# GpSimd takes the smaller of two scores for even groups too, ScalarE writes the queries' high part, the per-pair work stands elsewhere

## Chip, core and metric

One core of a Trainium2 chip runs the whole program. The metric is the device time of one execution in microseconds (us); several executions were timed, and another one was profiled.

## What is computed

Three stages follow one another. The change lies in the first, attention in which each query keeps only its 32 largest scores:

```python
def _attn_ref(q, k, v):                      # q, k, v: (4, 8, 576, 64)
    scores = scale * np.matmul(q, k.transpose(0, 1, 3, 2))
    kth = np.partition(scores, -32, axis=-1)[..., -32:-32 + 1]
    scores = np.where(scores >= kth, scores, -1000000000.0)
    attn = np.exp(scores - np.max(scores, axis=-1, keepdims=True))
    attn = attn / (np.sum(attn, axis=-1, keepdims=True) + 1e-09)
    return np.matmul(attn, v)
```

Its output goes token by token to one of eight experts (`h = max(x @ w1[e], 0)`, `out = gate * (h @ w2[e])`), and then through one dense layer pair with a piecewise quadratic function in between. Those two stages are untouched.

## The kernel before

The 32 heads are taken in 16 pairs. A pair has nine score tiles ("units") of 128 queries by 576 keys, so there are 144 units, worked off in 72 groups g of two. Each pass of the loop over g (L503) writes out, engine by engine, one group's selection (`topk`, L238), the masks and the product with v of the groups before it, and the scores of group g + 4 (`AHEAD`). Every engine runs its own instructions in the order in which they were written; only data and buffers make it wait.

**The selection.** VectorE finds the 32 largest of 576 with an instruction that gives the eight largest of a row (MAX8) and one that strikes these out (MATCH_REPLACE8). To shorten the rows, a *fold* (`fold`, L209) first halves them: `big` is the larger of column i and column i + 288 (L215), `c` the larger of the two halves of `big` (L216), `lit2` the smaller of them (L217). One fold serves four units, that is two groups: it is made in each odd group g for the groups g + 1 and g + 2. The smaller values of the first halving, `lit`, have two makers. For even groups VectorE makes them with one minimum (`smaller`, L222). For odd groups GpSimd does, as the exact integer sum of both columns (L230) less the larger one (L235); this is `less`, and a dependency written by hand lets it start only behind VectorE's L222. The groups of `DIRECT` keep VectorE. Then come three pairs of MAX8, over `lit2` (L253), over `lit` (L255) and over `c` with the best eight of each appended (L257), in an odd group the fold, and three rounds of MATCH_REPLACE8 (L266, its MATCH_VALUE_LOAD ahead of it) and MAX8 (L269). GpSimd makes the exponent's bias `nm` from the first maximum (L258) and copies two small results, `edge` and `top` (L242), when it comes to the next group.

**The per-pair work.** Scores are made from split operands, so each pair needs k and q transposed (`turn`, ScalarE copies kT and qT from PSUM, L170), the rounded high parts kh (VectorE, `kparts`, L174) and qh (GpSimd, `qparts`, L182), and the rests kl and ql (GpSimd, `krest` L178, `qrest` L186). `prep` sets the groups: turns in g - 2, kh in g - 1, the rest in g, with g odd (L393): 3, 7, 13, 17, 21, 25, 31, 35, 39, 43, 49, 53, 57, 61; the work of pair 1 stands in group 0. TensorE multiplies with them from L197 to L199, and ScalarE evacuates a unit's scores with L207.

**The output of a pair** (`xout`, L338) is scaled by VectorE's L343 and L344 and a product on GpSimd, in the odd groups 7, 11, 17, 21, 25, 29, 35, 39, 43, 47, 53, 57 and 61 for the first 13 pairs. In groups 66 to 68 GpSimd scatters token rows to DRAM (five, five and three).

Of the kernel before, what the change touches and what calls it, by code (L numbers as in the profile page):

```python
# [11 lines left out]
AF = mybir.ActivationFunctionType  # L12
ALU = mybir.AluOpType
# [33 lines left out]
AHEAD = 4  # L47
LEAVE = 3
START = (0, 1, 1, 2, 2, 3)
DIRECT = (67, 71)  # L50
FIRST = (0, 4, 9, 13)
NT1 = FIRST[B - 1]
SEG = ((0, 512), (512, S))
# [12 lines left out]
class Kernel:  # L66
# [32 lines left out]
    def attention(self, moe):  # L99
        nc, tc = self.nc, self.tc  # L100
        with ExitStack() as ctx:
            P = self.P
# [11 lines left out]
            def nb(n):  # L114
                return n if P.deep else 1
# [21 lines left out]
            raw, kq, st, xr = {}, {}, {}, {}  # L137
# [5 lines left out]
            def load(j, other=nc.sync):  # L143
                for nm, src, queue in (("k", self.k, nc.sync), ("q", self.q, other)):
                    t = raw[nm, j] = P.kq.tile([128, 5, 2, D], F32, name="r" + nm, bufs=nb(2))
                    for i, hd in enumerate(heads(src, j)):
                        queue.dma_start(t[:, 0:4, i, :],
                                          hd[:, :, 0:512, :].rearrange("a b (p c) d -> p (a b c) d", c=4))
                        queue.dma_start(t[0:64, 4, i, :],
                                          hd[:, :, 512:S, :].rearrange("a b p d -> p (a b d)"))  # L150

            def load_v(j, t):
                for i, hd in enumerate(heads(self.v, j)):
                    nc.sync.dma_start(t[:, i, 0:4, 0:D],
                                      hd[:, :, 0:512, :].rearrange("a b (p c) d -> p (a b c) d", c=4))
                    nc.sync.dma_start(t[64:128, i, 4, 0:D],
                                      hd[:, :, 512:S, :].rearrange("a b p d -> p (a b d)"))

            def vtile(j):
                return P.V[j % len(P.V)]  # L160

            def turn(j, nm):
                r = raw.pop((nm, j))
                p = P.sp.tile([128, 1024], F32, name="sp")
                for c in range(5):
                    n = 128 if c < 4 else 64
                    nc.tensor.transpose(p[:, c * 128:c * 128 + n],
                                        r[:n, c].rearrange("p h d -> p (h d)"), self.ident[:n, :n])
                t = kq[nm, j] = P.kq.tile([128, S], F32, name=nm + "T", bufs=nb(2))
                nc.scalar.activation(t, p[:, :S], AF.Copy)  # L170

            def kparts(j):
                hi = kq["kh", j] = P.kq.tile([128, S], F32R, name="kh", bufs=nb(2))
                nc.vector.tensor_copy(hi, kq["k", j])  # L174

            def krest(j, eng=nc.gpsimd):
                lo = kq["kl", j] = P.kq.tile([128, S], F32R, name="kl", bufs=nb(2))
                eng.tensor_tensor(lo, kq["k", j], kq["kh", j].bitcast(F32), op=ALU.subtract)  # L178

            def qparts(j):  # L180
                t, (hi, lo) = kq["q", j], P.Q[j % len(P.Q)]
                nc.gpsimd.tensor_tensor(hi, t[:, 0:512], P.zero, op=ALU.add)  # L182

            def qrest(j, eng=nc.gpsimd):
                t, (hi, lo) = kq["q", j], P.Q[j % len(P.Q)]
# [23 lines left out]
            def fold(s):  # L209
                h, q = S // 2, S // 4  # L210
                n = s.shape[1]
                big = P.wk.tile([128, n, h], F32, name="big", bufs=1)
                c = P.wk.tile([128, n, q + 16], F32, name="c")
                lit2 = P.wk.tile([128, n, q], F32, name="lit2", bufs=1)
                nc.vector.tensor_tensor(big, s[:, :, 0:h], s[:, :, h:S], op=ALU.max)  # L215
                nc.vector.tensor_tensor(c[:, :, 0:q], big[:, :, 0:q], big[:, :, q:h], op=ALU.max)  # L216
                nc.vector.tensor_tensor(lit2, big[:, :, 0:q], big[:, :, q:h], op=ALU.min)  # L217
                return [[t[:, i:i + 2] for t in (c, lit2, big)] for i in range(0, n, 2)]

            def smaller(g):  # L220
                lits[g] = P.wk.tile([128, 2, S // 2], F32, name="lit")
                return nc.vector.tensor_tensor(lits[g], st[g][:, :, 0:S // 2], st[g][:, :, S // 2:S], op=ALU.min)  # L222

            folded, lits, moved = {}, {}, []

            def less(g, behind):

                i = st[g].bitcast(I32)
                t = P.wk.tile([128, 2, S // 2], I32, name="lit")
                d = nc.gpsimd.tensor_tensor(t, i[:, :, 0:S // 2], i[:, :, S // 2:S], op=ALU.add)  # L230

                tc.add_manual_dep(d.ins, behind.ins.name,
                                  mybir.DependencyInfo(mybir.DependencyClass.Sync, mybir.DependencyReason.DATA),
                                  reason="shared port")
                nc.gpsimd.tensor_tensor(t, t, folded[g][2].bitcast(I32), op=ALU.subtract)  # L235
                lits[g] = t.bitcast(F32)

            def topk(g):  # L238
                q = S // 4
                two = range(2)  # L240
                while moved:
                    nc.gpsimd.tensor_copy(*moved.pop(0))  # L242
                if g < 2:
                    folded[g], = fold(st[g])
                if g not in lits:
                    smaller(g)
                c, lit2, _ = folded.pop(g)
                lit = lits.pop(g)
                m8 = P.wk.tile([128, 2, TOPK // 8, 8], F32, name="m8", bufs=4)
                z = P.wk.tile([128, 2, q + 16], F32, name="z", bufs=1)  # L250
                nm = P.wk.tile([128, 2], F32, name="nm", bufs=4)
                for i in two:
                    nc.vector.max(c[:, i, q + 8:q + 16], lit2[:, i])  # L253
                for i in two:
                    nc.vector.max(c[:, i, q:q + 8], lit[:, i])  # L255
                for i in two:
                    nc.vector.max(m8[:, i, 0], c[:, i])  # L257
                nc.gpsimd.tensor_scalar(nm, m8[:, :, 0, 0], -0.125, None, op0=ALU.mult)  # L258
                if g % 2 and g + 1 < ng:
                    folded[g + 1], folded[g + 2] = fold(four[g // 2 + 1])  # L260
                    behind = smaller(g + 1)
                    if g + 2 not in DIRECT:
                        less(g + 2, behind)
                for r in range(TOPK // 8 - 1):
                    for i in two:
                        nc.vector.match_replace(out=z[:, i], in_to_replace=m8[:, i, r],  # L266
                                                in_values=c[:, i] if r == 0 else z[:, i], imm_value=LOWEST)
                    for i in two:
                        nc.vector.max(m8[:, i, r + 1], z[:, i])  # L269
                last = m8[:, :, TOPK // 8 - 1, 7:8]  # L270
                moved.append((edge[:, 2 * g:2 * g + 2], c[:, :, q + 7::8]))
                moved.append((top[:, 2 * g:2 * g + 2], last[:, :, 0]))
                return [(last[:, i], nm[:, i:i + 1]) for i in two]
# [88 lines left out]
            ng = nu // 2  # L362
            later = {}

            def at(g, f, *a):
                later.setdefault(max(g, 0), []).append((f, a))

            def odd(g):
                return g if g % 2 else g - 1

            def prep(j, g, *eng):

                at(g - 2, turn, j, "k")
                at(g - 2, turn, j, "q")
                at(g - 1, kparts, j)
                at(g, krest, j, *eng)
                at(g, qparts, j)
                at(g, qrest, j, *eng)

            load(0, nc.scalar)  # L380
# [9 lines left out]
            at(1, self.route_consts)  # L390
            at(5, self.route_consts2)
            for j in range(1, len(pairs)):
                g = odd(9 * j // 2 - AHEAD - 1)  # L393
                prep(j, g)
                if j + 1 < len(pairs):
                    at(g - 2, load, j + 1)
# [191 lines left out]
            def again(j):  # L588
                load(j)
                load_v(j, vtile(j))  # L590
                for nm in "kq":
                    turn(j, nm)
                kparts(j)
                krest(j)
                qparts(j)
                qrest(j)
                for u in range(9):
                    s = P.wk.tile([128, S], F32, name="s1", bufs=1)
                    sevac(s, qk(j, u))
                    t, nm = topk_plain(s)  # L600
                    work = [(j, u, ptevac(pt(ex(s, nm), wmask(s, t))))]
                    avevac(work, av(work))
                xout(j)
# [1136 lines left out]
```

## Time and profile before

| | |
|---|---|
| median of 3 timed runs | 1214.36 us (1214.07 to 1219.26) |
| profiled execution, its own time | 1211.65 us |
| its span, first to last instruction | 1210.0 us |
| mean granted TensorE clock | 0.962 of full speed |
| busy: TensorE, VectorE, ScalarE, GpSimd | 1119.0, 842.0, 693.8, 499.6 us |
| attention | up to some 515 us |

A row of the timeline gives the start, the duration and the instruction; in brackets stands how long its engine had been idle before it, and what ended that. "x2" merges two instructions of a kind. Consecutive instructions of VectorE overlap by some 0.08 us, so what one costs its queue is the step from its start to the next start. A duration also holds the time in which an instruction that had been issued was held up.

### The profile page before, as it was taken

Reading aid. Unit: us, or ns where it says so; the run is one execution under the profiler, and the core shown is the slowest. Engines: PE = TensorE matmul, PEld = TensorE weight load, DVE = VectorE, ACT = ScalarE, POOL = GpSimd, SP = SyncE. Lnnn points to the kernel's source line nnn. Section 1 sums busy time; section 2 is a strip of 40 time slices with the busy share of each in tenths; the row PEclk is TensorE's granted clock in tenths of the full one; section 3 lists DMA queues with packets and bytes.
Section 4 is the critical chain, followed back from the end, with each engine's and each line's share of the span. In section 5 each row is a group of like instructions: output and inputs, shape, how many; then the busy total and the mean of one; then the engine's idle time right before and its main releaser. Section 6 shows DMA issues by size and latency. Waiting matters only on the chain. (4 is left out here: it accounts for less than half of the span.)

```text
span 1210.0 us, 24589 instructions
## 1 busy us (share of the span) xinstructions
PE 1119.0 (92%) x8900; PEld 955.7 (79%) x8901; DVE 842.0 (70%) x2572; ACT 693.8 (57%) x1230; POOL 499.6 (41%) x621
## 2 busy tenths in 40 slices
PE   8987989899989898777999999889899999999997
PEld 5776878677878776666888787778799999999996
DVE  6999999999999999886757888477422232322222
ACT  4878888898889886733655544345333333333322
POOL 2555556555555555752224445132232322222221
PEclk7899999999999998997999999899899999999999
DMA  4126573112011102354876565133000101000000
GB/s 90 31 82 204 170 224 116 31 31 51 12 31 36 26 18 84 132 183 131 268 222 220 165 225 180 59 132 103 27 27 18 35 1 44 9 35 18 28 1 27
DMA packets 120846, 106.70 MB, mean 88 GB/s; under 512 B 64384, under 2 KB 88960, under 8 KB 120704
## 3 DMA queue, kind: packets, MB, share of 16 engines
q1 hardware_dynamic: 115888, 93.10, 24.8%
q0 software_dynamic: 3312, 11.01, 2.7%
q8 instruction: 74, 1.21, 0.4%
q10 hardware_dynamic: 1504, 0.82, 0.2%
q14 instruction: 68, 0.56, 0.1%
HBM read 70.30 MB, written 34.60 MB: 87 GB/s over the span
## 5 line engine op out<-in xcount | busy, mean ns | idle before, releaser
L1216 POOL TENSOR_TENSOR gl<-g,gh 128x384 fp32r<-128x384 f32 x96 | 97.1, 1011 | 299.7 <-ACT gh L1215 262.6
L1210 ACT ACTIVATE c<-c,half 128x384 f32<-128x384 f32 x96 | 59.3, 618 | 172.3 <-DVE c L1209 172.3
L1209 DVE TENSOR_SCALAR c<-h 128x384 f32<-128x384 f32 x95 | 52.7, 555 | 150.4 <-PE h L1065 150.4
L305 PE MATMUL tp<-nhuge,w 128*128 128x128 bf16 x720 | 137.6, 228 | 16.5 <-ACT w L294 16.5
L303 PE MATMUL tp<-ident,e 128*128 128x128 f32 x720 | 148.9, 299 | 2.7 <-ACT e L289 2.7
L1062 PE MATMUL h<-xh,wih 128*128 128x384 f32 x380 | 131.8, 347 | 7.7 <-ACT xh L1056 5.6
L1063 PE MATMUL h<-xh,wil 128*128 128x384 f32 x380 | 131.2, 345 | 0.0
L303 PEld LDWEIGHTS tp<-ident,e 128*128 128x128 f32 x720 | 106.9, 148 | 29.8 <-issue 8.6
L1381 POOL TENSOR_TENSOR w1l<-w1r,w1h 128x512 fp32r<-128x512 f32 x48 | 66.8, 1393 | 128.3 <-ACT w1h L1380 102.6
L269 DVE MAX8 m<-z 128x8 f32<-128x160 f32 x432 | 117.2, 313 | 0.0
L310 ACT ACTIVATE a<-tp 128x640 f32<-128x640 f32 x144 | 101.7, 706 | 22.8 <-PE tp L305 20.7
L1073 PE MATMUL y<-woh,gl 128*128 128x512 f32 x288 | 114.0, 396 | 0.4 <-POOL gl L1216 0.4
L1071 PE MATMUL y<-woh,gh 128*128 128x512 f32 x288 | 112.1, 389 | 2.1 <-ACT gh L1215 2.1
L1072 PE MATMUL y<-wol,gh 128*128 128x512 f32 x288 | 113.7, 395 | 0.0
L1213 DVE TENSOR_TENSOR g<-c,h 128x384 f32<-128x384 f32 x95 | 52.5, 553 | 85.6 <-ACT c L1210 85.6
L294 ACT ACTIVATE w<-s,m 128x576 bf16<-128x576 f32 x144 | 103.5, 770 | 14.5 <-DVE m L269 14.5
L289 ACT ACTIVATE e<-s,nm 128x576 f32<-128x576 f32 x144 | 103.2, 767 | 14.2 <-POOL nm L258 14.1
L207 ACT ACTIVATE s<-sp 128x576 f32<-128x576 f32 x144 | 92.6, 644 | 25.1 <-PE sp L199 22.8
L197 PE MATMUL sp<-kh,qh 64*128 64x288 f32 x256 | 90.6, 361 | 15.4 <-POOL qh L182 13.9
L322 PE MATMUL tp<-v,a 128*64 128x65 f32 x2880 | 102.3, 226 | 0.0
L322 PEld LDWEIGHTS tp<-v,a 128*64 128x64 f32 x2880 | 92.2, 140 | 12.8 <-issue 6.2
L305 PEld LDWEIGHTS <-w 128*128 128x128 bf16 x720 | 80.8, 113 | 19.6 <-ACT w L294 19.4
(323 smaller groups left out, 2906.4 us busy)
## 6 DMA issues: line engine op xcount, KB each, us to landing
w1r<-in_moe_w_dram SPq DMA_DIRECT2D x56, 256.0 KB, 3.6
w2r<-in_moe_w_dram SPq DMA_DIRECT2D x56, 256.0 KB, 3.2
xs_dr<-zero SPq DMA_DIRECT2D x19, 512.0 KB, 4.8
ys_dr<-zero SPq DMA_DIRECT2D x19, 512.0 KB, 5.5
cr<-in_moe_w_in_dram SPq DMA_DIRECT2D x16, 512.0 KB, 4.7
cr<-in_moe_w_out_dram SPq DMA_DIRECT2D x13, 512.0 KB, 3.2
rows<-xs_dr SPq DMA_DIRECT2D x20, 256.0 KB, 2.8
ys_dr<-rows SPq DMA_DIRECT2D x17, 256.0 KB, 2.2
```

What stands on the lines that cost most here:

```text
L269: nc.vector.max(m8[:, i, r + 1], z[:, i])
L289: nc.scalar.activation(e, s, AF.Exp, bias=nm, scale=0.125)
L294: nc.scalar.activation(w, s, AF.Relu, bias=t, scale=-1.0)
L303: nc.tensor.matmul(o, e[:, k0:k0 + 128], self.ident, is_transpose=True, start=True, stop=False)
L305: nc.tensor.matmul(o, w[:, k0:k0 + 128], self.nhuge, start=False, stop=True)
L310: nc.scalar.activation(a, p[:, 0:640], AF.Relu)
L322: nc.tensor.matmul(o[HS[i]], a[:, k0:k0 + 64], v_[:, u % 2 if u < 8 else i, kc, :], start=kc == 0, stop=kc == 4)
L1062: nc.tensor.matmul(p, wh[c], xh[:, c, :], start=c == 0, stop=False)
L1063: nc.tensor.matmul(p, wl[c], xh[:, c, :], start=False, stop=False)
L1071: nc.tensor.matmul(y[t], hh[:, o], wh, start=first, stop=False)
L1072: nc.tensor.matmul(y[t], hh[:, o], wl, start=False, stop=False)
L1073: nc.tensor.matmul(y[t], hl[:, o], wh, start=False, stop=last)
```

## The change

Three things are changed. GpSimd makes `lit` for the even groups as well: in an odd group for g + 1, behind the last operation of the fold, and in the even group g + 1 for g + 2, with no dependency written by hand; groups 67, 68, 70 and 71 keep VectorE's minimum. qh is no longer made by GpSimd: ScalarE writes it from PSUM in `turn`, right after qT. And `prep` uses even groups: 4, 8, 12, 16, 22, 26, 30, 34, 40, 44, 48, 52, 58 and 62, with kh one group earlier and the turns two; pair 1 stays in group 0.

```diff
@@ -47,7 +47,7 @@
 AHEAD = 4
 LEAVE = 3
 START = (0, 1, 1, 2, 2, 3)
-DIRECT = (67, 71)
+DIRECT = (67, 68, 70, 71)
 FIRST = (0, 4, 9, 13)
 NT1 = FIRST[B - 1]
 SEG = ((0, 512), (512, S))
@@ -168,6 +168,8 @@
                                         r[:n, c].rearrange("p h d -> p (h d)"), self.ident[:n, :n])
                 t = kq[nm, j] = P.kq.tile([128, S], F32, name=nm + "T", bufs=nb(2))
                 nc.scalar.activation(t, p[:, :S], AF.Copy)
+                if nm == "q":
+                    nc.scalar.activation(P.Q[j % len(P.Q)][0], p[:, :512], AF.Copy)
 
             def kparts(j):
                 hi = kq["kh", j] = P.kq.tile([128, S], F32R, name="kh", bufs=nb(2))
@@ -176,10 +178,6 @@
             def krest(j, eng=nc.gpsimd):
                 lo = kq["kl", j] = P.kq.tile([128, S], F32R, name="kl", bufs=nb(2))
                 eng.tensor_tensor(lo, kq["k", j], kq["kh", j].bitcast(F32), op=ALU.subtract)
-
-            def qparts(j):
-                t, (hi, lo) = kq["q", j], P.Q[j % len(P.Q)]
-                nc.gpsimd.tensor_tensor(hi, t[:, 0:512], P.zero, op=ALU.add)
 
             def qrest(j, eng=nc.gpsimd):
                 t, (hi, lo) = kq["q", j], P.Q[j % len(P.Q)]
@@ -214,7 +212,7 @@
                 lit2 = P.wk.tile([128, n, q], F32, name="lit2", bufs=1)
                 nc.vector.tensor_tensor(big, s[:, :, 0:h], s[:, :, h:S], op=ALU.max)
                 nc.vector.tensor_tensor(c[:, :, 0:q], big[:, :, 0:q], big[:, :, q:h], op=ALU.max)
-                nc.vector.tensor_tensor(lit2, big[:, :, 0:q], big[:, :, q:h], op=ALU.min)
+                P.behind = nc.vector.tensor_tensor(lit2, big[:, :, 0:q], big[:, :, q:h], op=ALU.min)
                 return [[t[:, i:i + 2] for t in (c, lit2, big)] for i in range(0, n, 2)]
 
             def smaller(g):
@@ -223,15 +221,16 @@
 
             folded, lits, moved = {}, {}, []
 
-            def less(g, behind):
+            def less(g, behind=None):
 
                 i = st[g].bitcast(I32)
                 t = P.wk.tile([128, 2, S // 2], I32, name="lit")
                 d = nc.gpsimd.tensor_tensor(t, i[:, :, 0:S // 2], i[:, :, S // 2:S], op=ALU.add)
-
-                tc.add_manual_dep(d.ins, behind.ins.name,
-                                  mybir.DependencyInfo(mybir.DependencyClass.Sync, mybir.DependencyReason.DATA),
-                                  reason="shared port")
+                if behind:
+
+                    tc.add_manual_dep(d.ins, behind.ins.name,
+                                      mybir.DependencyInfo(mybir.DependencyClass.Sync, mybir.DependencyReason.DATA),
+                                      reason="shared port")
                 nc.gpsimd.tensor_tensor(t, t, folded[g][2].bitcast(I32), op=ALU.subtract)
                 lits[g] = t.bitcast(F32)
 
@@ -258,9 +257,12 @@
                 nc.gpsimd.tensor_scalar(nm, m8[:, :, 0, 0], -0.125, None, op0=ALU.mult)
                 if g % 2 and g + 1 < ng:
                     folded[g + 1], folded[g + 2] = fold(four[g // 2 + 1])
-                    behind = smaller(g + 1)
-                    if g + 2 not in DIRECT:
-                        less(g + 2, behind)
+                    if g + 1 in DIRECT:
+                        smaller(g + 1)
+                    else:
+                        less(g + 1, P.behind)
+                elif g and g + 1 < ng and g + 1 not in DIRECT:
+                    less(g + 1)
                 for r in range(TOPK // 8 - 1):
                     for i in two:
                         nc.vector.match_replace(out=z[:, i], in_to_replace=m8[:, i, r],
@@ -374,7 +376,6 @@
                 at(g - 2, turn, j, "q")
                 at(g - 1, kparts, j)
                 at(g, krest, j, *eng)
-                at(g, qparts, j)
                 at(g, qrest, j, *eng)
 
             load(0, nc.scalar)
@@ -390,7 +391,7 @@
             at(1, self.route_consts)
             at(5, self.route_consts2)
             for j in range(1, len(pairs)):
-                g = odd(9 * j // 2 - AHEAD - 1)
+                g = odd(9 * j // 2 - AHEAD) - 1
                 prep(j, g)
                 if j + 1 < len(pairs):
                     at(g - 2, load, j + 1)
@@ -592,7 +593,6 @@
                     turn(j, nm)
                 kparts(j)
                 krest(j)
-                qparts(j)
                 qrest(j)
                 for u in range(9):
                     s = P.wk.tile([128, S], F32, name="s1", bufs=1)
```

On VectorE, in an odd group with a fold (group 17 of the program), there stands before, from the last MAX8 pair to the first round:

```order
L257 MAX m_1728<-c 128x8 x2
L215 TENSOR_TENSOR big<-s 128x1152
L216 TENSOR_TENSOR c<-big 128x4x144
L217 TENSOR_TENSOR lit_1740<-big 128x576
L222 TENSOR_TENSOR lit<-s 128x576
L266 MATCH_REPLACE z<-m_1728,c 128x160 x2
```

and in the changed program, whose line numbers differ by one or two:

```order
L256 MAX m_1738<-c 128x8 x2
L213 TENSOR_TENSOR big<-s 128x1152
L214 TENSOR_TENSOR c<-big 128x4x144
L215 TENSOR_TENSOR lit_1750<-big 128x576
L268 MATCH_REPLACE z<-m_1738,c 128x160 x2
```

The minimum behind the fold is gone; VectorE has 2084 rows in place of 2117.

On GpSimd, around the work of pair 4, there stands before (group 17, odd, up to the nm of group 18; m is the maxima that nm, edge and top read):

```order
L258 TENSOR_SCALAR nm<-m_1728 128x2
L230 TENSOR_TENSOR lit<-s 128x576
L235 TENSOR_TENSOR lit<-lit,big 128x576
L178 TENSOR_TENSOR kl<-kT,kh 128x576
L182 TENSOR_TENSOR qh_115<-qT,zero 128x512
L186 TENSOR_TENSOR ql_116<-qT,qh_115 128x512
L242 COPY edge<-c 128x4
L242 COPY top<-m_1728 128x2
L258 TENSOR_SCALAR nm<-m_1846 128x2
```

and now (group 16, even, up to the pair of operations of group 17):

```order
L257 TENSOR_SCALAR nm<-m_1633 128x2
L228 TENSOR_TENSOR lit<-s 128x576
L234 TENSOR_TENSOR lit<-lit,big 128x576
L180 TENSOR_TENSOR kl<-kT,kh 128x576
L184 TENSOR_TENSOR ql_116<-qT,qh_115 128x512
L241 COPY edge<-c 128x4
L241 COPY top<-m_1633 128x2
L257 TENSOR_SCALAR nm<-m_1738 128x2
L228 TENSOR_TENSOR lit<-s 128x576
L234 TENSOR_TENSOR lit<-lit,big 128x576
```

qh has left the queue, kl and ql stand one group elsewhere, behind an even group's pair of lit operations that was not there, and each group has its own pair.

## Rows read from the trace of the kernel before

**Rows 1.** Stretches: busy us (instructions) of PE, PEld, DVE, ACT, POOL; clock, DMA.

```profile
30.00:500.00 470.00, 423.52 (x5330) 351.65 (x5330) 464.89 (x1895) 392.24 (x692) 264.55 (x399) 0.95 0.26 79
600.00:1200.00 600.00, 583.75 (x2854) 512.73 (x2853) 284.40 (x431) 238.65 (x423) 184.77 (x163) 0.99 0.25 81
```

**Rows 2.** Timeline of VectorE (start, duration), odd group 17 from its first MAX8.

```profile
135.30 0.51 DVE L253 MAX8 c<-lit 128x8 f32<-128x144 f32 x2
135.73 0.80 DVE L255 MAX8 c<-lit 128x8 f32<-128x288 f32 x2
136.45 0.53 DVE L257 MAX8 m<-c 128x8 f32<-128x160 f32 x2
136.90 1.33 DVE L215 TENSOR_TENSOR big<-s 128x1152 f32<-128x1152 f32 x1
138.34 0.76 DVE L216 TENSOR_TENSOR c<-big 128x576 f32<-128x576 f32 x1
...
139.68 0.75 DVE L222 TENSOR_TENSOR lit<-s 128x576 f32<-128x576 f32 x1
140.35 0.09 DVE L266 MATCH_VALUE_LOAD z<-m,c 128x8 f32 x1
...
143.48 0.16 DVE L343 TENSOR_SCALAR r<-xr 128x9 f32<-128x9 f32 x1
```

**Rows 3.** Timeline of GpSimd, even group 16 (first row) and odd group 17.

```profile
131.99 0.21 POOL L258 TENSOR_SCALAR nm<-m 128x2 f32<-128x2 f32 x1 [1.43 <-DVE m L257]
...
137.06 1.25 POOL L258 TENSOR_SCALAR nm<-m 128x2 f32<-128x2 f32 x1 [1.64 <-DVE m L257]
140.61 1.41 POOL L230 TENSOR_TENSOR lit<-s 128x576 int32<-128x576 int32 x1 [2.30 <-DVE lit L222]
142.10 1.43 POOL L235 TENSOR_TENSOR lit<-lit,big 128x576 int32<-128x576 int32 x1
143.47 1.46 POOL L178 TENSOR_TENSOR kl<-kT,kh 128x576 fp32r<-128x576 f32 x1
144.89 1.27 POOL L182 TENSOR_TENSOR qh<-qT,zero 128x512 fp32r<-128x512 f32 x1
```

**Rows 4.** Timelines of VectorE and GpSimd in group 1, where both run two-input operations.

```profile
22.20 0.75 DVE L215 TENSOR_TENSOR big<-s 128x576 f32<-128x576 f32 x1
22.99 1.54 DVE L216 TENSOR_TENSOR c<-big 128x288 f32<-128x288 f32 x1
24.45 1.51 DVE L217 TENSOR_TENSOR lit<-big 128x288 f32<-128x288 f32 x1
...
22.37 1.84 POOL L178 TENSOR_TENSOR kl<-kT,kh 128x576 fp32r<-128x576 f32 x1 [5.30 <-DVE kh L174]
24.18 1.48 POOL L182 TENSOR_TENSOR qh<-qT,zero 128x512 fp32r<-128x512 f32 x1
```

**Rows 5.** Timelines of VectorE and GpSimd in even group 12, behind an output product.

```profile
105.22 0.54 DVE L257 MAX8 m<-c 128x8 f32<-128x160 f32 x2
...
106.34 0.22 POOL L258 TENSOR_SCALAR nm<-m 128x2 f32<-128x2 f32 x1
```

**Rows 6.** Timeline of VectorE at the end of odd group 21.

```profile
169.93 1.43 DVE L343 TENSOR_SCALAR r<-xr 128x9 f32<-128x9 f32 x1
```

**Rows 7.** Timelines of ScalarE and GpSimd at the start, first pair.

```profile
7.75 0.65 ACT L170 ACTIVATE qT<-sp 128x576 f32<-128x576 f32 x1
...
8.49 1.53 POOL L182 TENSOR_TENSOR qh<-qT,zero 128x512 fp32r<-128x512 f32 x1 [6.63 <-ACT qT L170]
```

**Rows 8.** Timelines of ScalarE and VectorE: last scores for a fold, and that fold.

```profile
306.42 0.64 ACT L207 ACTIVATE s<-sp 128x576 f32<-128x576 f32 x1
...
309.68 1.34 DVE L215 TENSOR_TENSOR big<-s 128x1152 f32<-128x1152 f32 x1
```

**Rows 9.** Timeline of GpSimd between the scatters, groups 67 and 68.

```profile
479.37 1.39 POOL L230 TENSOR_TENSOR lit<-s 128x576 int32<-128x576 int32 x1
...
490.16 0.76 POOL L258 TENSOR_SCALAR nm<-m 128x2 f32<-128x2 f32 x1
```

## The prediction

> **What bounds the kernel now.** I first read the stretches [rows 1]. From 30 to 500 us, the attention, VectorE is busy for 464.9 of 470 us, TensorE for 423.5 and ScalarE for 392.2; from 600 us on it is TensorE, 583.8 of 600. So in the attention one group of two score tiles takes as long as VectorE's instructions for it, and what comes behind is TensorE work that starts when the attention ends and should shift with it, since nothing in it is touched. Then I read VectorE's queue through one odd group [rows 2] and GpSimd's beside it [rows 3]. The reader is to see start-to-start steps: 0.43 (L253), 0.72 (L255), 0.45 (L257), then the fold, 1.44 (L215), 0.67, 0.67 and L222's 0.67, then three rounds of match_replace and max, 3.13 together. An even group has no fold.
>
> The next thing to see is which of the two engines stops the other. L230 and L235 run on GpSimd for 1.41 and 1.43 us beside the match_replace rounds, and these take the same 3.13 as elsewhere: no conflict. Two-input operations of both do conflict [rows 4]: L216, 128x288, takes 1.54 us, because GpSimd's kl (22.37, 1.84 long) ends only at 24.21, and L217 (1.51) then waits for the next GpSimd operation, which had itself waited for L216. They take turns, whole operations at a time. Even the tiny nm of an odd group is held by L215: 1.25 us against 0.21 in an even group [rows 3].
>
> **The change, part by part.** The sum is made against the profiled execution, 1211.65 us (span 1210.0). The median of the timed runs is 1214.36, 2.7 more, and I add that at the end. M is the start of a group's match_replace rounds.
>
> *Removed from VectorE.* 33 of 39 L222 go (even groups 2 to 66; VectorE has 33 rows fewer in the program). Each is a step of 0.67, from L222 to the rounds [rows 2], all on the path: 33 x 0.67 = **-22.1**.
>
> *Added to GpSimd.* 33 more pairs of operations, 1.41 + 1.43 each [rows 3]. Their cover is the rounds. In an even group nm starts 0.62 behind L257, that is M+0.17; the pair follows at M+0.33 and M+1.81 and ends near M+3.23. VectorE needs the result at M+3.13+0.43 = M+3.56. In an odd group the pair starts behind L217 where it stood behind L222, 0.26 after the rounds begin, and ends at M+3.18. So there is a margin of 0.3 to 0.4 us, taken as cost 0. If each pair were 0.2 us beyond the margin, 66 groups would pay 13 us; that is the upper bound, and a rival below.
>
> *The xout groups.* Behind 13 odd groups GpSimd also multiplies the output, and so its nm of the next even group comes late: at 106.34, 1.12 behind L257 at 105.22 instead of 0.62 [rows 5]. The pair then ends near M+3.7, and with some 0.1 for the signal VectorE waits about 0.25: 13 x 0.25 = **+3.3** (0 to 6.5).
>
> *The per-pair work.* kl and ql used to stand in odd groups, where a whole even group without a fold followed. Now they stand behind the pair of an even group (14 times; the 15th is at the start), and the next thing on VectorE is the fold of the odd group. The steps from the pair's second operation (L235) to kl and from kl to qh are 1.37 and 1.42, and ql, of qh's size, takes 1.27 [rows 3]. So kl runs from M+3.2 to M+4.6 and ql from M+4.5 to M+5.8, but L215 is due at M+3.13+0.43+0.72+0.45 = M+4.73. Taking turns as in [rows 4], either L215 waits 1.1 us for ql, or (behind an xout) L215 slips in at 0.1 late and L216 waits 1.1 for ql. The small copies edge and top, which used to be out of the way, then get a turn each at about 0.1 as they pass between the fold's operations. Cost 1.1 + 0.15 = 1.25 each, 14 x 1.25 = **+17.5**. The bounds: 0.9 (no turn for the copies, ql 0.2 earlier), 12.6, and 1.8 (both kl and ql in the way for a part), 25.
>
> A rule speaks against moving work here at all. What the rows show is that GpSimd disturbs the fold and not the rounds [rows 2 to 4]. The Trainium skill, "Perfetto Trace Analysis", section "Optimizing Scalar/DVE Operations", says that moving operations between VectorE and GpSimd might not help because they share a port; by that the new pairs would be paid for as kl and ql are, which is rival (d). The same skill's "SBUF — State Buffer", section "Who interferes with whom", leaves VectorE instructions with one SBUF input outside the two-port modes undisturbed; the trace agrees with this one, by the unchanged 3.13 us.
>
> *qh leaves GpSimd.* In the groups it hid beside the rounds, so nothing on the path goes with it, except three times: L343, which waits in an odd group for whatever GpSimd holds, takes 1.43 us at 169.93 [rows 6] and 0.16 at 143.48 [rows 2]. Three of 13 do this, each behind the start of kl, which is not there any more: 3 x 1.27 = **-3.8** (0 if timed runs don't show it). ScalarE gets 16 more copies of at most 0.65 (as the qT copy [rows 7]), 10 us, or 402 of some 465: covered. At the start it is on the path: qT ends at 8.40, GpSimd's qh runs 8.49 to 10.02, while ScalarE's would end near 8.95: **-1.1**. In group 1 the turns of [rows 4] are one fewer: **-1.1**. qh no longer fills a queue that TensorE waits for.
>
> *kh one group earlier.* Its cast now comes just as the pair's end leaves the port: 14 times 0 to 0.1, **+0.7**.
>
> *Scores in time.* For half of the pairs kl and ql now come one group later, so TensorE can stand for 3 us. What hides this is that scores are made ahead: the last evacuation before the fold at 309.68 ends at 307.06, 2.6 us ahead [rows 8], one of the tighter places. **+1.0** (0 to 8).
>
> *The tail.* At 479.37 the pair for group 69 runs ahead of five scatters; now it stands one group later, behind them and behind nm (490.16) [rows 9]. nm and the exponentials gain what VectorE then loses waiting, 2.9 us; both meet again at ScalarE's masks. **+0.5** (0 to 2.9).
>
> Sum: -22.1 - 3.8 - 2.2 + 17.5 + 3.3 + 0.7 + 1.0 + 0.5 = **-5.1**. That is 1206.5 on the profiled execution and **1209.3** against the median.
>
> **The rivals.** (a) *Most of the relief stays.* GpSimd's steps turn out 0.1 to 0.2 shorter, the xout wait vanishes and ql costs 0.9: -22.1 - 3.8 - 2.2 + 12.6 + 0.5 = -15.0, 1199. For it: the margins are tenths of a us. Against it: GpSimd's durations vary by hundredths. (b) *GpSimd becomes the path*: slower than before. L255 waits for the pair in every group, from the point where the pair ends over 0.35 us later than reckoned; at 0.2 beyond it, +13 on -5.1 gives +8, 1222. For it: GpSimd's spans are rough, and nm, edge and top stand ahead of the pair in one queue. Against it: in before the odd groups' pair meets the same deadline at L343 by 0.05 without harm. (c) *Scores come late.* The 3 us of TensorE show in the eight late pairs where the lead is under 3 to 5 us: up to +8 in place of +1, 1216. (d) *The new pairs hold VectorE*: each of the 33 stretches the rounds by one turn of 1.1 us, +36 on -5.1, 1245; the pairs that already run there speak against it.
>
> **How the numbers follow.** Forecast 0.55, (a) 0.20, (b) 0.11, (c) 0.12, (d) 0.02. The forecast's own range is 1205 to 1214. The range for 8 in 10 takes in (a) and (c) and most of (b): 1199 to 1221. A measurement of this kernel tells some 0.5% (6 us) from no change: faster is under 1208.3, slower over 1220.4. Faster has (a) and a bit over a third of the forecast, 0.40; slower has most of (b) and (d), 0.12; within 0.5% is left with 0.48, and it is where the forecast lies, at -0.4%.
>
> **What would show it.** Right: six L222 remain; of the fold in 14 odd groups one operation (L215 or L216 of before) is 1.1 us longer than its 1.33 or 0.75; L255's line gains idle time ending with GpSimd's second operation, some 0.25 in 13 places; L343 is 0.15 throughout; the first score is evacuated 1.1 us earlier; VectorE stays over 98% busy, with more of it spent in held operations. Wrong: idle time ahead of L255 in most groups (b), or ahead of L215 with ScalarE's evacuation as releaser (c), or a fold that is never held (a). If the attention ends 5 us earlier and the total doesn't follow, the step from the attention's end to the end of the kernel was wrong.

## The result and the profile after

The changed kernel takes 1200.47 us (median of 4 runs, 1194.8 to 1202.59), the kernel before 1216.13 (4 runs, 1214.07 to 1219.26). The ratio is 0.9861, with a 95% interval of 0.9833 to 0.9889: 1.4% faster, where the prediction held a gain of 0.4%, too small to be told from none, to be likeliest. The time lies inside the predicted range and at its lower part. The two profiled executions, 1211.65 and 1201.56 us, are only 10.1 us apart. So there are two things to explain: why that pair shows 10 and not 5, and why the medians show some 16.

Line numbers of the kernel after are mostly two lower or higher: L215 to L217 of before are L213 to L215, L222 is L220, L253 and L255 are L252 and L254, L343 is L345, L230 and L235 are L228 and L234. "Pair" means the two GpSimd operations of L228 and L234, "group" two score tiles, "fold" L213 to L215.

The stretches of the kernel after (busy us with instruction counts of TensorE, its weight loads, VectorE, ScalarE, GpSimd; then clock, DMA share, GB/s), to be held against [rows 1]:

```profile
30.00:490.00 460.00, 428.00 (x5324) 354.58 (x5323) 453.11 (x1857) 399.91 (x707) 348.05 (x450) 0.95 0.27 83
600.00:1190.00 590.00, 572.80 (x2783) 502.75 (x2783) 279.85 (x421) 231.12 (x408) 180.61 (x161) 0.99 0.23 76
```

VectorE is still what bounds the attention, busy for 453.1 of 460 us, and GpSimd went from 56% to 76%. The groups of VectorE's instructions in the kernel after, by line, from 25 to 470 us (busy us, mean ns, idle us before them and what ended it), and VectorE's waits from 30 to 505 us (us, times, longest):

```profile
L254 DVE MAX8 c<-lit 128x8 f32<-128x288 f32 x134 | 54.0, 444 | 2.5 <-POOL lit L234 2.3
L213 DVE TENSOR_TENSOR big<-s 128x1152 f32<-128x1152 f32 x34 | 50.0, 1469 | 0.0
L214 DVE TENSOR_TENSOR c<-big 128x576 f32<-128x576 f32 x34 | 35.3, 1039 | 1.3
L345 DVE TENSOR_SCALAR r<-xr 128x9 f32<-128x9 f32 x14 | 2.3, 166 | 0.0
L220 DVE TENSOR_TENSOR lit<-s 128x576 f32<-128x576 f32 x3 | 2.2, 749 | 0.0
...
DVE c L254 <- POOL lit L234: 4.1, 12, 1.9
DVE r L345 <- POOL top L550: 2.5, 1, 2.5
```

Three things are to be read here. L220 is nearly gone (3 in this stretch, 6 in all, 39 before). The means of L213 and L214 have risen from the 1.33 and 0.76 of [rows 2] to 1.47 and 1.04: some of them are held. And what VectorE waits for from GpSimd is little: 4.1 us, 1.9 of it at one place in the tail.

Which ones are held shows in an odd group behind a pair's work, first VectorE, then GpSimd (start, duration, in brackets the idle time before it and what ended that):

```profile
78.70 0.82 DVE L254 MAX8 c<-lit 128x8 f32<-128x288 f32 x2 [0.16 <-POOL lit L234]
...
79.90 1.36 DVE L213 TENSOR_TENSOR big<-s 128x1152 f32<-128x1152 f32 x1
81.29 1.71 DVE L214 TENSOR_TENSOR c<-big 128x576 f32<-128x576 f32 x1
82.93 0.75 DVE L215 TENSOR_TENSOR lit<-big 128x576 f32<-128x576 f32 x1
...
78.63 1.41 POOL L180 TENSOR_TENSOR kl<-kT,kh 128x576 fp32r<-128x576 f32 x1
80.00 2.39 POOL L184 TENSOR_TENSOR ql<-qT,qh 128x512 fp32r<-128x512 f32 x1
82.34 0.71 POOL L241 COPY edge<-c 128x4 f32<-128x4 f32 x1
```

ql, 1.27 us when nothing is in its way (so qh, of its size, in [rows 3]), is held by L213 and lasts 2.39, and L214 is held by ql: 1.71 for 0.76. This is the taking of turns that [rows 4] showed in group 1. It happens in 14 odd groups. In ten, those behind an output product, it is L214 that is held (1.70 to 1.72). In the four others ql starts first, and L213 is held (2.37 to 2.40 for 1.34), as here in group 5:

```profile
51.43 2.37 DVE L213 TENSOR_TENSOR big<-s 128x1152 f32<-128x1152 f32 x1
...
51.30 1.29 POOL L184 TENSOR_TENSOR ql<-qT,qh 128x512 fp32r<-128x512 f32 x1
```

**Where the time of the pair of profiles went**, by the starts of VectorE's first MAX8 in a group. Group 1 starts at 25.09 instead of 27.64 (-2.55). From there to group 66 it is 431.22 us instead of 440.52 (-9.3). Groups 66 to 71 take 35.09 instead of 33.58 (+1.5). What lies behind group 71 is equal, 708.22 and 708.29.

### The profile page after: what moved, and what is told of

Read it like the earlier page. It is cut to its first block, busy times and chain, and to the rows that moved or that the text cites. A ratio compares the mean times of both kernels' runs of the same rounds, so it can differ in the third digit from the quotient of the medians.

```text
span 1199.6 us, 24610 instructions
## 1 busy us (share of the span) xinstructions
PE 1125.7 (94%) x8900; PEld 960.3 (80%) x8901; DVE 832.4 (69%) x2539; ACT 702.7 (59%) x1246; POOL 581.7 (48%) x671
## 5 line engine op out<-in xcount | busy, mean ns | idle before, releaser
L305 PE MATMUL tp<-ident,e 128*128 128x128 f32 x720 | 152.8, 302 | 0.0
L228 POOL TENSOR_TENSOR lit<-s 128x576 int32<-128x576 int32 x66 | 93.4, 1415 | 30.7 <-DVE lit L215 24.5
```

The source lines that it names most:

```text
L305: nc.tensor.matmul(o, e[:, k0:k0 + 128], self.ident, is_transpose=True, start=True, stop=False)
```

## The experiments

Theory A was the walk through VectorE's queue by which the prediction was made, with the sizes that the profile after showed: L222 less, 14 folds held, little else. Theory B said that something further, which the pair of profiles doesn't show, gives 5 to 6 us more. Theory C said that the moving of the per-pair work matters little.

**Both kernels again.** Unchanged, first with several timed executions of each, later as single profiled ones.

> The changed kernel once more, against the kernel before on the same chip. Theory A (the walk through VectorE's queue: 22.1 us of L222 and 3.8 of L343 removed, 2.5 won at the start, some 16 paid back where kl and ql meet the fold, 1.5 lost in the tail): the two profiled executions differ by 10.1 us, so the timed ratio should be near 0.992. Theory B (there is a further gain of 5 to 6 us that the two profiles don't show): the ratio stays at 0.986 to 0.988.

> The kernel before, unchanged, as a second profile of it. Theory A: VectorE's queue is the same but for the number of L343 that wait behind kl (3 of 13 in the first profile); each more costs 1.3 us, so with all 13 waiting the attention ends 12.7 us later. If unprofiled executions of before have more such waits, the time of before is 3 to 8 us over the 1211.65 of the profiled one and this profile shows 5 to 9 waits. Theory B: the number of waits stays 3 and the difference lies behind the attention. Ratio 1.00.

> The kernel before, unchanged: one more profiled execution, to see what differs between its executions (1211.65 and 1220.77 us profiled so far). Theory A: between the end of group 1 and the start of group 71 two things alone differ, the number of the 128x9 L343 that wait behind kl's start on GpSimd (3 and 5 so far, 1.27 us each) and groups 66 to 71 (33.6 and 37.6 us, the longer with TensorE's granted clock at 0.84 against 0.93 there and two waits of L343 for ScalarE's xr); a third execution has 3 to 10 such waits and one of the two ends, the time follows from them within 1.5 us. Rival: the difference lies elsewhere, in single groups of VectorE's queue or behind group 71 (708.3 and 709.7 us so far).

> The kernel before, unchanged: a fourth profiled execution. The same as for before_p1: 3 to 10 of the 128x9 L343 held 1.27 us each, and groups 66 to 71 in 33 to 34 us or in 37 to 38 us.

> The kernel after, unchanged: a third profiled execution. Theory A: no 128x9 L345 over 0.3 us, the same 14 long folds in the same groups, 12 waits for lit, groups 66 to 71 in 35 us, so that from group 1 to group 71 it agrees with the two others (466.3 and 468.5 us) within 2.5 us, less than the executions of before differ (474.1 and 481.6 us).

After: 1200.75 us, ratio 0.9859 (0.9834 to 0.9883). Before: 1219.76, ratio 1.0003 (0.9979 to 1.0026). So the gap of the medians is real, and A, which expected 0.992, was wrong on it. The profiled executions tell where it lies (us between starts of VectorE's groups; "held" counts the 128x9 L343 or L345 over 1.3 us):

| execution | its time | start to group 1 | 1 to 66 | 66 to 71 | behind 71 | held |
|---|---|---|---|---|---|---|
| before, the one predicted from | 1211.65 | 27.64 | 440.52 | 33.58 | 708.29 | 3 |
| before_again | 1220.77 | 27.87 | 443.97 | 37.62 | 709.67 | 5 |
| before_p1 | 1214.83 | 27.85 | 439.28 | 34.11 | 711.94 | 2 |
| before_p2 | 1218.08 | 27.80 | 441.31 | 37.54 | 709.79 | 3 |
| after | 1201.56 | 25.09 | 431.22 | 35.09 | 708.22 | 0 |
| after_again | 1202.45 | 23.92 | 433.41 | 35.12 | 708.04 | 0 |
| after_p1 | 1202.81 | 23.95 | 434.10 | 35.09 | 707.69 | 0 |

The execution that the prediction was made from was the shortest of the four; their mean is 1216.3, that of the three of after 1202.3, 14.1 less. Between group 1 and group 66 before's executions differ as A said: 2, 3, 3 and 5 held L343, each step 1.24 to 1.30 longer, and in before_again and before_p2 one step (group 53, where VectorE waits 0.6 us for scores) 0.7 longer. Two held was fewer than expected, and before_p1 is 3.7 us longer behind group 71 than the first, which A left out. In the tail two of them are 4 us longer. The stretch around groups 69 to 71, first in the execution predicted from, then in before_again with VectorE's two waits there:

```profile
490.00:516.00 26.00, 20.27 (x275) 16.54 (x277) 19.66 (x85) 20.36 (x37) 17.92 (x36) 0.93 0.33 105
```

```profile
494.00:525.00 31.00, 27.94 (x343) 22.62 (x342) 19.34 (x85) 21.55 (x39) 17.73 (x34) 0.84 0.27 87
...
500.84 0.17 DVE L343 TENSOR_SCALAR r<-xr 128x9 f32<-128x9 f32 x1 [1.83 <-ACT xr L336]
...
508.52 0.17 DVE L343 TENSOR_SCALAR r<-xr 128x2 f32<-128x2 f32 x1 [2.33 <-ACT xr L333]
```

With the granted clock of TensorE at 0.84 in place of 0.93, the products that xr is copied from come late, and VectorE stands. In before_again the clock is 0.50, the lower of its two levels (1.2 GHz), from 492 to 503 us; in the 4 us before, TensorE had been busy for 0.4. In the execution predicted from it is at that level from 494 to 497 us only. In the kernel after this tail took 35.1 us in all three, at a granted clock of 1.00 from 480 to 504 us. The stretch behind group 71 is 1.9 us shorter in the mean, and that part is not explained; nor is the rest of the difference between the mean of the profiled executions (14.1 us) and the medians (15.7 and, on the chip of after_again, 18.3).

The kernel after has a variation of its own: groups 25 to 29 took 3.0 us more in after_again than in after. The stretch in after, then in after_again with VectorE's waits from 170 to 205 us:

```profile
180.00:190.00 10.00, 9.79 (x112) 8.38 (x112) 9.96 (x41) 8.97 (x19) 6.58 (x7) 1.00 0.60 165
```

```profile
180.00:190.00 10.00, 9.76 (x75) 7.82 (x71) 8.93 (x34) 5.59 (x11) 4.99 (x7) 0.60 0.41 92
...
DVE big L213 <- ACT s L205: 1.8, 1, 1.8
DVE kh L176 <- ACT kT L170: 1.0, 1, 1.0
```

TensorE ran 75 instructions in these 10 us instead of 112, at a granted clock of 0.60, and the lead of the scores (2.6 us, [rows 8]) was not enough. From 175 to 185 us the clock was at the lower level, 0.50. From 165 to 170 us, at 1.00, TensorE had been busy for 3.0 of 5 us; but in after it was busy for 3.1 of 5 us from 170 to 175, and the clock stayed at 1.00, so what made it fall is not shown. The expectation for after_p1, agreement within 2.5 us, was missed by a little (2.9): VectorE waits for the scores in group 63 (1.9 us) and for xr in group 64 (1.8), and so 13 folds are held there and not 14.

**The selection alone.** The kernel before with GpSimd's pair for even groups (less, fold and DIRECT as in the change); qh stays on GpSimd, the per-pair work where it was.

```
-                    behind = smaller(g + 1)
-                    if g + 2 not in DIRECT:
-                        less(g + 2, behind)
+                    if g + 1 in DIRECT:
+                        smaller(g + 1)
+                    else:
+                        less(g + 1, P.behind)
+                elif g and g + 1 < ng and g + 1 not in DIRECT:
+                    less(g + 1)
```

> The changed selection alone: GpSimd makes lit for all groups, but qh stays on GpSimd and the per-pair work stays in odd groups. Theory A: kl, qh and ql (4 us) now stand between an odd group's pair and the next even group's pair, whose result is due some 5.1 us behind the first pair's end; VectorE's L254 waits about 2.3 us, and 3 to 4 where the output product also stands there, in 14 groups: 40 to 45 us paid for 22 won, so 15 to 22 us slower than before, ratio 1.012 to 1.019. Theory C (moving the per-pair work matters little, the relief of VectorE is the gain): ratio 0.985 to 0.99.

1231.76 us, ratio 1.0108 (1.0078 to 1.0137): slower, as A expected and C did not, but by 12.7 us and not by A's 15 to 22. VectorE's wait and its 128x9 L347 (L343 of before), 30 to 470 us:

```profile
DVE c L256 <- POOL lit L236: 31.6, 14, 2.4
...
L347 DVE TENSOR_SCALAR r<-xr 128x9 f32<-128x9 f32 x13 | 14.6, 1122 | 0.0
```

In 14 odd groups the pair comes 2.0 to 2.4 us late behind kl, qh and ql, 31.6 us together where A had 40 to 45. Ten L347 are held, which A had not reckoned with. The part that takes 22 us off VectorE's queue makes the kernel slower by itself: what it removes it gives back as waits, because the room on GpSimd has to be made first.

**qh on ScalarE alone.** The kernel before with qh written from PSUM.

```
+                if nm == "q":
+                    nc.scalar.activation(P.Q[j % len(P.Q)][0], p[:, :512], AF.Copy)
...
-                at(g, qparts, j)
```

> The kernel before with qh written by ScalarE and nothing else changed. Theory A: only the start (-1.1) and group 1 (-1.1) are on the path, ratio 0.998. Theory B (TensorE gets its operands earlier, 14 us of waits for qh, and that is the part of the gain that the walk lacks): ratio 0.993 to 0.996.

1213.19 us, ratio 0.9966 (0.9946 to 0.9986), between A's 0.998 and B's 0.993 to 0.996, so it doesn't tell them apart. Group 1 starts at 23.94 us instead of 27.6 to 27.9, which is 3.9 of the 4.4 us by which its profiled execution (1211.90) lies below the mean of before's four. The medians are 5.9 us apart, within an interval of 1.7 to 6.6. The held L343 are still there, five of them, so it is not qh's leaving that removes them:

```profile
L341 DVE TENSOR_SCALAR r<-xr 128x9 f32<-128x9 f32 x14 | 8.5, 607 | 0.0
```

**The third part undone.** The kernel after, the per-pair work at the odd groups again.

```
-                g = odd(9 * j // 2 - AHEAD) - 1
+                g = odd(9 * j // 2 - AHEAD - 1)
```

> After with its third part alone undone: the per-pair work stands at the odd groups where the kernel before has it, behind GpSimd's smaller for the even group; the smaller of even groups and the queries' high part on ScalarE stay. Theory A (the third part buys the even groups' room): in less_only the lit of 14 odd groups came 2.1 to 2.4 us late behind kl, qh and ql; without qh (1.36 us) it comes 0.7 to 1.1 us late, 14 x 0.9 = 13 us, and kl starts as VectorE runs its 128x9 L345, which was held 1.27 us in 10 pairs of less_only: together 22 to 26 us, against 13.4 for the folds and 2 for lit that after pays: 7 to 10 us slower than after, 1207 to 1211 us, ratio to before 0.991 to 0.994; VectorE's wait for lit at odd groups 10 to 15 us in 14 waits. Theory C (moving the per-pair work matters little): within 3 us of after, ratio 0.983 to 0.989.

1209.57 us, ratio 0.9969 (0.9954 to 0.9984). That is by the ratios 13 us slower than after (after itself was not run on that chip), by the table's stretch from 1 to 66 (440.93 us) 7 to 10. The time and the stretch are as A had them, the ratio is above its 0.991 to 0.994. C falls. VectorE's wait and L345, 30 to 470 us:

```profile
DVE c L254 <- POOL lit L234: 12.5, 14, 1.0
...
L345 DVE TENSOR_SCALAR r<-xr 128x9 f32<-128x9 f32 x14 | 14.8, 1057 | 0.0
```

Both terms are there as expected: 12.5 us in 14 waits, and ten L345 held by 1.25, some 12.5; no fold is held. The place that the change chose costs 14 held folds and 2 us of waits instead. With the selection as in after, moving the work exchanged 25 us for 16.

This run differs from less_only by qh alone. With qh off GpSimd the waits for the pair fall from 31.6 to 12.5 us and the ratio from 1.0108 to 0.9969. So qh's leaving, worth 0.3% by itself, is worth 1.4% once the selection stands on GpSimd. The selection with the moved work but with qh on GpSimd was not run.

**The held folds taken away.** The kernel after with ql two groups earlier than kl (one group in three of the 14 places), each alone behind a pair. What then stands ahead of the fold, one operation and not two, ends as the fold starts.

```
+                early = j % 4 != 1 and j > 0
-                at(g - 2, turn, j, "k")
-                at(g - 2, turn, j, "q")
+                at(g - 2 - early, turn, j, "k")
+                at(g - 2 - early, turn, j, "q")
...
-                at(g, qrest, j, *eng)
+                at(g - 1 - early if j > 1 else g, qrest, j, *eng)
```

> After, with the per-pair subtractions taken apart: ql two groups earlier than kl, each alone in an even group's slot on GpSimd, so that neither lies beside VectorE's fold (the turns of the queries and keys onto PSUM go one or two groups earlier with them). Theory A (14 folds of after are each held about 0.96 us because GpSimd's ql is still running: L213 2.37 to 2.40 for 1.34, L214 1.70 to 1.72 for 0.76): the 14 long folds go, 14 x 0.96 = 13.4 us less, given back at most 0.15 us in the 7 to 13 groups with an x output ahead, where kl still ends as the fold starts: 12 us faster than after, 1188 to 1190 us, ratio to before 0.974 to 0.977, no L213 over 1.6 us and no L214 over 1.0 us in a pair's group. Theory C (the holds are covered by something else that is late anyway, the scores or the selection's lit): within 3 us of after, ratio 0.983 to 0.989, and the time of the folds turns up as a wait of VectorE on ScalarE (s L205) or GpSimd (lit).

1184.63 us (before 1214.1 on that chip), ratio 0.9761 (0.9737 to 0.9785), which is the ratio that A expected. The fold from 25 to 470 us, and GpSimd and VectorE at one of the 14 places:

```profile
L213 DVE TENSOR_TENSOR big<-s 128x1152 f32<-128x1152 f32 x35 | 47.2, 1349 | 0.0
L214 DVE TENSOR_TENSOR c<-big 128x576 f32<-128x576 f32 x35 | 26.6, 760 | 1.3
...
74.90 1.42 POOL L180 TENSOR_TENSOR kl<-kT,kh 128x576 fp32r<-128x576 f32 x1
...
76.18 1.36 DVE L213 TENSOR_TENSOR big<-s 128x1152 f32<-128x1152 f32 x1
77.58 0.76 DVE L214 TENSOR_TENSOR c<-big 128x576 f32<-128x576 f32 x1
```

kl ends at 76.32, 0.14 into L213, which costs 0.02 (1.36 for 1.34). Group by group against after_again, 13 of the 14 steps shrink by 0.95 to 1.06 us each; the 14th, group 27, is left out, because its fold waited 1.8 us for the scores in after_again. Outside groups 25 to 29 no other step between group 1 and 71 differs by more than 0.02. So a held fold, with the small waits around it, cost 1.01 us of the whole, 14.2 for the 14.

**The tail's wait.** The same, with group 69 taken by VectorE again.

```
-DIRECT = (67, 68, 70, 71)
+DIRECT = (67, 68, 69, 70, 71)
```

> The same as slots, and the smaller of two scores of group 69 is taken by VectorE again (DIRECT gets 69 back; it costs VectorE 0.67 us), because in the profile of after L254 waits 1.9 us there for GpSimd, which issues the scatter's descriptors just ahead. Theory A (every gap of VectorE's queue counts one to one up to the end of the groups): 1.9 - 0.67 = 1.2 us faster than slots, 1187 to 1189 us, and no wait of L254 over 0.5 us behind 440 us. Rival D (behind group 69 the end is set by TensorE and ScalarE, the xr rows that L345 waits for, so that the wait is slack): equal to slots within 0.5 us, with a longer wait of L345 on ScalarE in groups 70 and 71.

1182.23 us, ratio 0.9731 (0.9706 to 0.9756), the best of these kernels. In the kernel after the wait stands behind a pair that GpSimd begins late:

```profile
474.54 1.40 POOL L228 TENSOR_TENSOR lit<-s 128x576 int32<-128x576 int32 x1
476.01 1.40 POOL L234 TENSOR_TENSOR lit<-lit,big 128x576 int32<-128x576 int32 x1
...
477.44 0.82 DVE L254 MAX8 c<-lit 128x8 f32<-128x288 f32 x2 [1.86 <-POOL lit L234]
```

In slots69 groups 66 to 71 take 33.90 us instead of 35.11 in slots: -1.2, as A had it (1.9 less 0.67). The timed difference of the two, 2.4 us, is within their intervals, so the profile alone carries that number.

**ql on VectorE.** The kernel after with the other engine for ql.

```
-                at(g, qrest, j, *eng)
+                at(g, qrest, j, nc.vector)
```

> After with ql (128x512, one per pair) on VectorE instead of GpSimd; kl stays where it is. Theory A: kl alone ends at the fold's start, so the long L213 and L214 go (13.4 us less), VectorE gets 14 subtractions of a step of 0.6 us each (0.67 per 128x576 in L215, by elements 512/576) = 8.4 us more, and up to 0.6 us each where kl still runs beside it: from 5 us faster to 3 us slower than after, 1196 to 1204 us, and no L214 over 1.0 us in a pair's group. Theory C: the folds were slack, so the subtractions come on top: 8 us slower, 1209 us.

1196.74 us, ratio 0.986 (0.983 to 0.989), that of after, inside A's bounds. One of the 14 places on both engines, and the group of ql, 25 to 470 us:

```profile
77.42 1.18 DVE L184 TENSOR_TENSOR ql<-qT,qh 128x512 fp32r<-128x512 f32 x1
...
76.65 1.41 POOL L234 TENSOR_TENSOR lit<-lit,big 128x576 int32<-128x576 int32 x1
78.02 1.86 POOL L180 TENSOR_TENSOR kl<-kT,kh 128x576 fp32r<-128x576 f32 x1
...
L184 DVE TENSOR_TENSOR ql<-qT,qh 128x512 fp32r<-128x512 f32 x14 | 15.1, 1075 | 0.0
```

The folds are free (L214 0.76 again), but ql on VectorE starts beside the pair's second operation, waits for its end at 78.06, and then holds kl in turn: 1.18 us. It moves the conflict by one instruction and pays about the same.

## Why the prediction was wrong

It missed the median by 8.8 us. Of these, 4.9 are the sum itself (-5.1 against -10.1 in the pair of profiles) and 3.9 the step from the profile to the median.

- **L222, -22.1: right.** 33 of 39 are gone, at one to one.
- **The held L343, -3.8: right for that execution, and put under the wrong part.** The three steps are 1.61 to 1.66 shorter where they stood (0.67 of it L222's, and 0.36 given back because kh's cast, which stood in the even group before, now stands in this one), and none is held in after. The prediction allowed for fewer of them in the timed runs; that there might be more (2 to 5 in four executions) it did not ask. And qh_only shows that qh's leaving removes none; it is the moving of kl.
- **The per-pair work, +17.5: the main step that was mis-sized.** The mechanism, the 14 places and even the two forms (L214 held behind an output product, L213 elsewhere) came as told. But a held fold costs 0.98 in the mean (0.95 for L214, 1.04 for L213) and not 1.1 + 0.15: 13.7 in all, and 14.2 when it is taken away. The two copies, put at 0.15, cost nothing: edge and top take 0.71 and 0.72 beside L214 and L215, which keeps its 0.75.
- **The pair's margin and the xout groups, 0 and +3.3: right, a bit too large.** Eleven waits up to group 66, 2.3 us together.
- **kh's cast, +0.7: 0** (0.36 less in the even group that it left, as much more in the odd one), and **the scores, +1.0: 0 in the first execution**, 3 us in each of the two others, where TensorE's clock was lower. This is rival (c), with the clock as its cause, which the prediction did not name.
- **The start, -2.2: -2.55 in the pair, -3.5 in the means.** ScalarE's qh ends at 8.84 us where GpSimd's ended at 10.02. Behind it, L222 of group 1 (L220 of after) takes 0.74 in place of 1.82, as qh's turn is gone. In after_again and after_p1 VectorE's wait for kT ahead of that, 1.65 us in after, is gone too.
- **The tail, +0.5: +1.5.** VectorE waits 1.86 us for group 69's pair, and only some 0.35 is saved beside it; from group 66 on both kernels run the same four L222.
- **Not foreseen:** in group 5 an int32 copy of VectorE lasts 1.54 us instead of the 0.40 that it takes in after_again, beside GpSimd's six iotas, +0.95 in the step. It starts just behind the first of them, in after by 0.08 us, in after_again by 0.07. after_p1, slots69 and ql_vector show the long copy too, before's four executions, old_prep and slots the short one; what decides it is not shown. After:

```profile
58.35 1.54 DVE L685 COPY mi<-mod 128x144 int32<-128x144 int32 x1
...
58.27 0.41 POOL L692 IOTA i<- 128x144 f32 x1
...
59.38 0.42 POOL L692 IOTA itab<- 128x152 f32 x1
```

The same copy in after_again:

```profile
57.19 0.40 DVE L685 COPY mi<-mod 128x144 int32<-128x144 int32 x1
```

From group 1 to 66 of the pair of profiles these measured terms give -22.1 - 3.8 + 13.7 + 2.3 + 0.9 = -9.0, against -9.3 between the rows.

**The step to the median** failed as a step of its own. The prediction added 2.7 us, as far as the median lay above the profiled execution, to its sum. But what differs between before's profiled executions is for the most part held L343 and TensorE's late xr in the tail, and neither appears in any of after's three. The timed executions were not profiled, so that the 2.7 were just these is argued and not shown. After's median lies 1.1 us below its own profiled execution. The execution that the sum was made against lay 4.7 us below the mean of four, so a gain counted from it had to come out small.

**The rivals.** (a) named almost the right time, 1199, in part by luck. Its 0.9 for ql is nearer to the measured 0.98 than the forecast's 1.25. But the waits behind xout did not vanish, the profiled execution would have been 1196.7 by its sum and was 1201.56, and its sign, a fold that is never held, does not fit its own 12.6 us for held folds; the folds are held in all 14 places. (b) did not occur: the pair is late by at most 0.3 us before the tail. (d) did not: the 66 pairs leave the match_replace rounds at 3.1 us, as in [rows 2]. The Trainium skill's rule from "Perfetto Trace Analysis", section "Optimizing Scalar/DVE Operations", that moving work between VectorE and GpSimd might not help, is borne out by less_only and ql_vector (1.0108, and 0.986 unchanged), though less_only loses most by the order of GpSimd's queue (31.6 us of waits). slots, at 0.9761, shows that it depends on what the moved operation runs beside.

## What to carry to other kernels

An operation moved between VectorE and GpSimd is free or paid for by where it lands: list what the other engine runs in that very slot, and count for each meeting of two-input operations what is left of the other one (here 0.98 us of ql's 1.27). Make the room first: here the part with the gain was a loss of 1.1% without the two that look like side work, and side work that is worth 0.3% alone was worth 1.4% beside it. And before a gain of a few us is summed, look at more than one profiled execution: count what differs between them, and ask whether the change removes just that.

## What the hardware showed that was not expected

- Two two-input operations that meet take turns, and the second loses what is left of the first (L214 1.71 for 0.76 beside ql, which takes 1.27 when free), but one that has only 0.14 us left to run costs 0.02 (slots, L213 1.36).
- An int32 copy of VectorE of 128x144 lasted 1.54 or 0.40 us in two executions of one program, started 0.08 and 0.07 us behind the first of six iotas on GpSimd; the long one ends just behind the last of them.
- Executions of one program had a granted TensorE clock of 1.00 or 0.60 in the same 10 us of the attention, and the engine with 98% busy time lost 3 us to it.
